# Loading and using the five row slices of w1 in the order 3, 4, 0, 1, 2 for the first chunk

## The chip, the cores and the metric

One core of one Trainium2 chip. The metric is the device time of a whole execution in microseconds (us). Profiles show the *span* from the first to the last instruction, which is about 1.8 us shorter than that time.

## The reference

```python
# x (1, 2048, 640), w1 (640, 1536), w2 (1536, 640), grad_out like x, all bf16
h   = x @ w1
out = silu(h) @ w2
# returned: out and the gradients of x, w1 and w2 for grad_out (by jax.vjp)
```

## The kernel before

The kernel takes x in four chunks of 512 rows. Per chunk it computes h (contraction over D = 640, that is, over five row slices of w1 with 128 rows each), silu and its derivative, out, and the gradients. Everything is bound by the matrix engine (TensorE); the only special place is the start, where w1 is still on its way from memory. For chunk 0 the code therefore works slice by slice: each slice of w1 that lands feeds 12 matmuls into six accumulators, for 256 of the 512 rows.

Loads, before anything else is awaited (`nc.sync` and `nc.scalar` are two queues that issue loads):

```python
early += [load_x(nc.sync, 0), load_x(nc.scalar, 1)]                     # 256 rows of x, natural layout
early += [load_w1(0, slice(0, F // 2)), load_w1(0, slice(F // 2, F), nc.scalar)]  # slice 0 in halves
early += [load_w1(k) for k in range(1, 3)]                              # slices 1, 2
for k in range(3, DT):                                                  # slices 3, 4
    load_w1(k)
nc.sync.dma_start_transpose(out=xT_next[:, :, HC:SC], in_=x2[HC:SC, :]) # the other 256 rows, transposed
# ... then w2, transposed grad_out, transposed w2 and w1, on the same queue
```

Transposing the first 256 rows on TensorE, and copying the five transposed column slices out in three pieces, on VectorE, ScalarE, VectorE:

```python
def pe_x(xT):
    slices = ((0, 1), (1, 3), (3, DT))
    tps = [ps_h.tile([P, hi - lo, 2, P], dt_in, ...) for lo, hi in slices]
    for q in range(2):
        for tp, (lo, hi) in zip(tps, slices):
            for dt_ in range(lo, hi):
                nc.tensor.transpose(tp[:, dt_ - lo, q, :], x_nat[:, q, dt_ * P:(dt_ + 1) * P], ident[:])
    for k, (tp, (lo, hi)) in enumerate(zip(tps, slices)):
        copy_tp = nc.scalar.copy if k % 2 else nc.vector.tensor_copy
        copy_tp(out=xT[:, lo:hi, 0:HC], in_=...)
```

The matmuls of chunk 0:

```python
def h_pair_mm(hp, pair, dt_, xT, cols, qs=(0, 1)):
    for q in qs:
        ft = 2 * pair + q
        nc.tensor.matmul(hp[:, q, :], lhsT=w1_nat[:, dt_, ft * P:(ft + 1) * P], rhs=xT[:, dt_, cols],
                         start=(dt_ == 0 and q == qs[0]), stop=(dt_ == DT - 1 and q == qs[-1]))

def h_first(xT, aT, ghT):
    pe_x(xT)
    ...
    for dt_ in range(DT):              # first 256 rows: slice by slice
        for pair in range(NPAIR):
            h_pair_mm(hs[0][pair], pair, dt_, xT, halves[0])
    ...                                # silu of the six accumulators
    for pair in range(NPAIR):          # other 256 rows: all slices have landed
        ...
        for q in range(2):
            for dt_ in range(DT):
                h_pair_mm(hp, pair, dt_, xT, halves[1], (q,))
```

Of the kernel before, what the change touches and what calls it, by code (L numbers as in the profile page):

```python
# [62 lines left out]
def kernel(  # L63
# [11 lines left out]
    nc = tc.nc  # L75
# [8 lines left out]
    F = w1.shape[1]  # L84
    ST, DT, FT = S // P, D // P, F // P
# [7 lines left out]
    NWARM = 18  # L93
    HC = 2 * P
    NPAIR = FT // 2
    NCOPY = 4
    dt_in = x.dtype

# [34 lines left out]
    with ExitStack() as mctx:  # L133
# [4 lines left out]
        tpool = mctx.enter_context(tc.tile_pool(name="tpool", bufs=3))  # L138
        hpool = mctx.enter_context(tc.tile_pool(name="hpool", bufs=NCOPY))
        opool = mctx.enter_context(tc.tile_pool(name="opool", bufs=2))  # L140

        warm = cpool.tile([P, P], dt_in, name="warm")
        early = [nc.vector.memset(warm[:], 1.0)]
# [25 lines left out]
        def load_x(eng, q):  # L169
            return eng.dma_start(out=x_nat[:, q, :], in_=x_v[:, q, :])  # L170

        def load_w1(k, cols=slice(0, F), eng=nc.sync):
            return eng.dma_start(out=w1_nat[:, k, cols], in_=w1_v[:, k, cols])  # L173

        early += [load_x(nc.sync, 0), load_x(nc.scalar, 1)]
        early += [load_w1(0, slice(0, F // 2)), load_w1(0, slice(F // 2, F), nc.scalar)]
        early += [load_w1(k) for k in range(1, 3)]
        for k in range(3, DT):
            load_w1(k)
        nc.sync.dma_start_transpose(out=xT_next[:, :, HC:SC], in_=x2[HC:SC, :])  # L180
        start_before_entry_wait(nc, {i.ins.name for i in early})
# [5 lines left out]
        nc.sync.dma_start_transpose(out=w1T[:], in_=w1[:, :])  # L187

        def pe_x(xT):
            slices = ((0, 1), (1, 3), (3, DT))  # L190
            tps = [ps_h.tile([P, hi - lo, 2, P], dt_in, name="tp", tag="hp") for lo, hi in slices]
            for q in range(2):
                for tp, (lo, hi) in zip(tps, slices):
                    for dt_ in range(lo, hi):
                        nc.tensor.transpose(
                            tp[:, dt_ - lo, q, :], x_nat[:, q, dt_ * P:(dt_ + 1) * P], ident[:]
                        )
            for k, (tp, (lo, hi)) in enumerate(zip(tps, slices)):
                copy_tp = nc.scalar.copy if k % 2 else nc.vector.tensor_copy
                copy_tp(out=xT[:, lo:hi, 0:HC], in_=tp[:].rearrange("p k q s -> p k (q s)"))  # L200
# [29 lines left out]
# [3 lines that stand above are left out]
                nc.tensor.matmul(  # L233
                    hp[:, q, :],
                    lhsT=w1_nat[:, dt_, ft * P:(ft + 1) * P],
                    rhs=xT[:, dt_, cols],
                    start=(dt_ == 0 and q == qs[0]),
                    stop=(dt_ == DT - 1 and q == qs[-1]),
                )

        def pair_silu(hp, pair, aT, cols):
            nc.scalar.activation(aT[:, 2 * pair:2 * pair + 2, cols], hp[:], ACT.Silu)

        def pair_grad(hp, pair, aT, ghT, cols):
            fts = slice(2 * pair, 2 * pair + 2)
            t = tpool.tile([P, 2, HC], FP32, name="t")
            nc.scalar.activation(t[:], hp[:], ACT.Tanh, scale=0.5)
            v = tpool.tile([P, 2, HC], dt_in, name="v")
            nc.vector.tensor_scalar(out=v[:], in0=t[:], scalar1=-0.5, scalar2=0.5, op0=ALU.mult, op1=ALU.add)
            nc.vector.scalar_tensor_tensor(  # L250
                out=ghT[:, fts, cols], in0=aT[:, fts, cols], scalar=1.0, in1=v[:],
                op0=ALU.subtract, op1=ALU.mult,
            )

        def h_first(xT, aT, ghT):
            pe_x(xT)
            halves = (slice(0, HC), slice(HC, SC))
            hs = [[ps_h.tile([P, 2, HC], FP32, name="hp") for _ in range(NPAIR)], []]
            for dt_ in range(DT):
                for pair in range(NPAIR):  # L260
                    h_pair_mm(hs[0][pair], pair, dt_, xT, halves[0])
            for pair in range(NPAIR):
                pair_silu(hs[0][pair], pair, aT, halves[0])
                if pair < NCOPY:
                    h_sb = hpool.tile([P, 2, HC], FP32, name="h_sb")
                    nc.vector.tensor_copy(out=h_sb[:], in_=hs[0][pair][:])
                    hs[0][pair] = h_sb
            grads = [(0, pair) for pair in list(range(NCOPY, NPAIR)) + list(range(NCOPY))]
            grads += [(1, pair) for pair in range(NPAIR)]
            for pair in range(NPAIR):  # L270
                hp = ps_h.tile([P, 2, HC], FP32, name="hp")
                hs[1].append(hp)
                for q in range(2):
                    for dt_ in range(DT):
                        h_pair_mm(hp, pair, dt_, xT, halves[1], (q,))
                pair_silu(hp, pair, aT, halves[1])
                if 1 <= pair <= 3:
                    half, done = grads.pop(0)
                    pair_grad(hs[half][done], done, aT, ghT, halves[half])
            for half, pair in grads:  # L280
                pair_grad(hs[half][pair], pair, aT, ghT, halves[half])
# [35 lines left out]
        for c in range(NCH):  # L317
# [15 lines left out]
            if c == 0:  # L333
                h_first(xT, aT, ghT)
                nc.sync.dma_start(
                    out=aT_scr[:, c * SC:(c + 1) * SC].rearrange("(ft p) s -> p ft s", p=P), in_=aT[:]
                )
                sd_phase(c, w2_nat, aT, oT_scr)
                for ft in range(FT):
                    g_group(ft, goT, ghT)  # L340
                nc.sync.dma_start(
                    out=ghT_scr[:, c * SC:(c + 1) * SC].rearrange("(ft p) s -> p ft s", p=P), in_=ghT[:]
                )
                sd_phase(c, w1T, ghT, gxT_scr)
                continue
# [20 lines left out]
    with ExitStack() as fctx:  # L366
# [17 lines left out]
        k = 0  # L384
        for fc in range(NFC):
            a_blk = a_blks[fc]
            g2T = fpool.tile([P, DT, FC], dt_in, name="g2T")
            for dt_ in range(DT):
                gp = ps_h.tile([P, FC], FP32, name="hp")
                for st in range(ST):  # L390
# [4 lines left out]
                        start=(st == 0),  # L395
                        stop=(st == ST - 1),
# [14 lines left out]
        k = 0  # L411
        for fc in range(NFC):
            gh_blk = gh_blks[fc]
            for dt_ in range(DT):
                if dt_ == DT // 2:
                    store_gw2(fc)
                if fc == NFC - 1 and dt_ == DT - 1:
                    for k, (lo, hi) in enumerate(((0, FC - P), (FC - P, FC))):
                        gp = ps_h.tile([P, FC], FP32, name="hp")
                        for st in range(ST):  # L420
# [4 lines left out]
                                start=(st == 0),  # L425
                                stop=(st == ST - 1),
# [12 lines left out]
                for st in range(ST):  # L439
# [4 lines left out]
                        start=(st == 0),  # L444
                        stop=(st == ST - 1),
# [38 lines left out]
```

## Time and profile before

| | value |
|---|---|
| time | 320.31 us, median of 3 runs (320.27 to 320.48) |
| span of the profiled run | 318.9 us |
| matmuls busy | 99% of the span |
| idle time of the matrix engine at w1 | 0.9 us in weight loads, all before 7.74 us |

The page's first part and its chain of waits, of the kernel before. In part 1 the columns are busy us, share of the span, number of instructions; PE is the matmuls of TensorE, PEld its weight loads, DVE VectorE, ACT ScalarE. The chain is what ended last, followed back to the start. (Names stand without numbers: `w_nat` is w1_nat or w2_nat, `hp` any accumulator.)

```profile
## 1 busy us (share of the span) xinstructions
PE 314.2 (99%) x1516; PEld 150.7 (47%) x1544; DVE 102.7 (32%) x182; ACT 76.8 (24%) x139; POOL 0.7 (0%) x6
...
## 4 chain that ended last, share of the span: by engine, by line
PE 96%; DMA 2%; issue 1%; SPq 0%; DVE 0%; DVEq 0%
PE hp L302 32%; PE hp L286 16%; PE hp L391 16%; PE hp L440 15%; PE hp L204 12%; PE hp L233 3%; DMA w_nat<-in_w_dram 2%; PE hp L421 1%; SPq L173 0%; SPq L170 0%; DVE g L432 0%; DVEq L432 0%; SPq L468 0%
```

So 96% of the span is TensorE one after another, and only 2% is a load, `w_nat<-in_w_dram`. Where that sits shows the chain of the first 20 us, in order of time (start us, duration us, what):

```profile
...
1.47 6.22 DMA w_nat<-in_w_dram
7.69 0.05 issue
7.74 10.65 PE hp L233 x96
...
```

The last thing that TensorE waited for was a load of w1 that landed at 7.69 us; from 7.74 us on the matmuls of h (L233) follow each other. The timeline of TensorE shows the pieces before that: first matmuls, then three groups of weight loads that each ended an idle time (in brackets: idle us, and what ended it).

```profile
...
2.59 1.25 PE L195 MATMUL tp<-ident,x_nat 128*128 128x128 bf16 x10
3.79 14.60 PE L233 MATMUL hp<-xT,w_nat 128*128 128x256 bf16 x120
...
```

```profile
...
3.53 1.22 PEld L233 LDWEIGHTS <-w_nat 128*128 128x128 bf16 x6
5.00 0.88 PEld L233 LDWEIGHTS <-w_nat 128*128 128x128 bf16 x6 [0.25 <-DMA w_nat<-in_w_dram]
6.18 1.21 PEld L233 LDWEIGHTS <-w_nat 128*128 128x128 bf16 x12 [0.30 <-DMA w_nat<-in_w_dram]
7.73 10.38 PEld L233 LDWEIGHTS <-w_nat 128*128 128x128 bf16 x96 [0.35 <-DMA w_nat<-in_w_dram]
...
```

The weight loads waited 0.25, 0.30 and 0.35 us for w1. The first of these was hidden: at that time matmuls started every 213 ns, where later they start every 109 ns, and the next one was not due yet. (The text below calls a step of 213 ns slow or half clock, and one of 109 ns full clock.) The other two are holes in the stream of matmuls.

### The profile page before, as it was taken

How to read it: one execution, taken by the hardware profiler on the slowest of the kernel's cores; microseconds unless marked ns; L12 is line 12 of the kernel's file. 1: busy time of each engine (PE TensorE's matmuls, PEld its weight loads, DVE VectorE, ACT ScalarE, POOL GpSimd, SP SyncE). 2: the span in 40 equal slices, each digit the busy share in tenths (PEclk: the TensorE clock that was granted, in tenths of full speed). 3: DMA queues.
4: the chain of work that ended last, by engine and by line, in shares of the span. 5: the costliest groups of instructions: out<-in, count | busy, mean ns of one | idle time of the engine just before them, and what ended most of it. 6: DMA issues, size and time to landing. Idle time of an engine off the chain costs nothing.

```text
span 318.9 us, 3632 instructions
## 1 busy us (share of the span) xinstructions
PE 314.2 (99%) x1516; PEld 150.7 (47%) x1544; DVE 102.7 (32%) x182; ACT 76.8 (24%) x139; POOL 0.7 (0%) x6
## 2 busy tenths in 40 slices
PE   9999999999999999999999999999999999999996
PEld 7854444444444444444444444444444444444443
DVE  1494641477410187710147741000000100001001
ACT  2691000644201354311064420111100001001100
POOL 0000000000000000000000000000000000000000
PEclk9999999999999999999999999999999999999999
DMA  8999999999999866492544089919999999996111
GB/s 268 311 177 222 216 266 255 313 270 304 260 232 342 201 191 174 144 299 82 164 120 128 0 268 265 210 38 290 222 258 255 228 214 339 229 311 216 38 39 45
DMA packets 147233, 67.02 MB, mean 210 GB/s; under 512 B 113937, under 2 KB 146705, under 8 KB 147217
## 3 DMA queue, kind: packets, MB, share of 16 engines
q1 hardware_dynamic: 146928, 66.43, 83.0%
q10 hardware_dynamic: 288, 0.36, 0.3%
q8 instruction: 12, 0.20, 0.3%
q14 instruction: 5, 0.03, 0.0%
HBM read 9.18 MB, written 28.97 MB: 120 GB/s over the span
## 4 chain that ended last, share of the span: by engine, by line
PE 96%; DMA 2%; issue 1%; SPq 0%; DVE 0%; DVEq 0%
PE hp L302 32%; PE hp L286 16%; PE hp L391 16%; PE hp L440 15%; PE hp L204 12%; PE hp L233 3%; DMA w_nat<-in_w_dram 2%; PE hp L421 1%; SPq L173 0%; SPq L170 0%; DVE g L432 0%; DVEq L432 0%; SPq L468 0%
## 5 line engine op out<-in xcount | busy, mean ns | idle before, releaser
L286 PE MATMUL hp<-goT,w2T 128*128 128x512 bf16 x239 | 56.8, 379 | 0.1
L302 PE MATMUL hp<-ghT,w1T 128*128 128x512 bf16 x235 | 52.2, 379 | 0.3
L302 PE MATMUL hp<-aT,w_nat 128*128 128x512 bf16 x234 | 52.1, 379 | 0.3
L391 PE MATMUL hp<-a_blk,go_nat 128*128 128x512 bf16 x235 | 51.7, 379 | 0.3
L440 PE MATMUL hp<-gh_blk,x_nat 128*128 128x512 bf16 x219 | 48.2, 379 | 0.3
L204 PE MATMUL hp<-xT,w_nat 128*128 128x512 bf16 x174 | 43.4, 379 | 0.3
L310 ACT ACTIVATE oT<-hp 128x512 bf16<-128x512 f32 x24 | 14.5, 604 | 106.8 <-PE hp L302 106.8
L302 PEld LDWEIGHTS <-w1T 128*128 128x128 bf16 x240 | 23.5, 98 | 28.3
L391 PEld LDWEIGHTS <-go_nat 128*128 128x128 bf16 x240 | 23.5, 98 | 28.3
L286 PEld LDWEIGHTS <-w2T 128*128 128x128 bf16 x240 | 23.5, 98 | 28.3
L302 PEld LDWEIGHTS <-w_nat 128*128 128x128 bf16 x240 | 23.5, 98 | 28.1
L293 DVE SCALAR_TENSOR_TENSOR ghT<-ghT,hp 128x512 bf16<-128x512 bf16 x48 | 32.5, 681 | 7.3 <-PE hp L286 7.3
L440 PEld LDWEIGHTS <-x_nat 128*128 128x128 bf16 x224 | 21.9, 98 | 26.4
L312 DVE CAST oT<-hp 128x512 bf16<-128x512 f32 x16 | 11.1, 691 | 72.2 <-PE hp L302 67.7
L213 ACT ACTIVATE aT<-hp 128x512 bf16<-128x512 f32 x36 | 21.5, 597 | 30.4 <-PE hp L204 30.4
L204 PEld LDWEIGHTS <-w_nat 128*128 128x128 bf16 x180 | 17.6, 98 | 21.3
L220 DVE SCALAR_TENSOR_TENSOR ghT<-aT,v 128x512 bf16<-128x512 bf16 x36 | 24.6, 684 | 0.2
L219 DVE TENSOR_SCALAR v<-t 128x512 bf16<-128x512 f32 x36 | 15.4, 426 | 26.7 <-ACT t L217 26.7
L217 ACT ACTIVATE t<-hp 128x512 f32<-128x512 f32 x36 | 21.3, 592 | 0.0
L451 DVE CAST g<-hp 128x512 bf16<-128x512 f32 x7 | 4.8, 691 | 47.0 <-PE hp L440 34.5
L401 DVE CAST g2T<-hp 128x512 bf16<-128x512 f32 x7 | 4.8, 692 | 46.1 <-PE hp L391 46.1
L399 ACT ACTIVATE g2T<-hp 128x512 bf16<-128x512 f32 x8 | 4.8, 597 | 47.0 <-PE hp L391 47.0
(28 smaller groups left out, 77.3 us busy)
## 6 DMA issues: line engine op xcount, KB each, us to landing
aT_scr<-aT SPq DMA_DIRECT2D x4, 1536.0 KB, 6.3
ghT_scr<-ghT SPq DMA_DIRECT2D x4, 1536.0 KB, 8.2
out_dram<-o_sb SPq DMA_DIRECT2D x8, 640.0 KB, 3.3
oT_scr<-oT SPq DMA_DIRECT2D x4, 640.0 KB, 3.6
go_nat<-in_grad_out_dram SPq DMA_DIRECT2D x4, 640.0 KB, 8.3
gxT_scr<-oT SPq DMA_DIRECT2D x4, 640.0 KB, 4.7
w_nat<-in_w_dram SPq DMA_DIRECT2D x1, 1920.0 KB, 11.1
x_nat<-in_x_dram SPq DMA_DIRECT2D x3, 640.0 KB, 7.2
```

The source lines that it names most:

```text
L204: nc.tensor.matmul(hp[:], lhsT=w1_nat[:, dt_, ft * P:(ft + 1) * P], rhs=xT[:, dt_, :], start=(dt_ == 0), stop=(dt_ == DT - 1),)
L213: nc.scalar.activation(aT[:, ft, :], hp[:], ACT.Silu)
L217: nc.scalar.activation(t[:], hp[:], ACT.Tanh, scale=0.5)
L219: nc.vector.tensor_scalar(out=v[:], in0=t[:], scalar1=-0.5, scalar2=0.5, op0=ALU.mult, op1=ALU.add)
L220: nc.vector.scalar_tensor_tensor(out=ghT[:, ft, :], in0=aT[:, ft, :], scalar=1.0, in1=v[:], op0=ALU.subtract, op1=ALU.mult)
L286: nc.tensor.matmul(gp[:], lhsT=w2T[:, dt_, ft * P:(ft + 1) * P], rhs=goT[:, dt_, :], start=(dt_ == 0), stop=(dt_ == DT - 1),)
L293: nc.vector.scalar_tensor_tensor(out=ghT[:, ft, :], in0=ghT[:, ft, :], scalar=1.0, in1=gp[:], op0=ALU.add, op1=ALU.mult)
L302: nc.tensor.matmul(op_[:], lhsT=w_all[:, ft, dt_ * P:(dt_ + 1) * P], rhs=rhs_all[:, ft, :], start=(ft == 0), stop=(ft == FT - 1),)
L310: nc.scalar.activation(oT[:, dt_, :], op_[:], ACT.Copy)
L312: nc.vector.tensor_copy(out=oT[:, dt_, :], in_=op_[:])
L391: nc.tensor.matmul(gp[:], lhsT=go_nat[:, st, dt_ * P:(dt_ + 1) * P], rhs=a_blk[:, st, :], start=(st == 0), stop=(st == ST - 1),)
L440: nc.tensor.matmul(gp[:], lhsT=x_nat[:, st, dt_ * P:(dt_ + 1) * P], rhs=gh_blk[:, st, :], start=(st == 0), stop=(st == ST - 1),)
```

## The change

The intent: use the slices of w1 in another order, and load them in that same order. Loads, transposes and matmuls of chunk 0 follow `KORD`; later chunks do not change. With it, the sizes of the copies of transposed x change from 1, 2, 2 slices to 1, 1, 3.

```diff
+    KORD = (3, 4, 0, 1, 2)
@@ loads
-        early += [load_w1(0, slice(0, F // 2)), load_w1(0, slice(F // 2, F), nc.scalar)]
-        early += [load_w1(k) for k in range(1, 3)]
-        for k in range(3, DT):
+        early += [load_w1(KORD[0], slice(0, F // 2)), load_w1(KORD[0], slice(F // 2, F), nc.scalar)]
+        early += [load_w1(k) for k in KORD[1:3]]
+        for k in KORD[3:]:
             load_w1(k)
@@ pe_x
-            slices = ((0, 1), (1, 3), (3, DT))
+            slices = ((3, 4), (4, DT), (0, 3))
@@ h_pair_mm
-                    start=(dt_ == 0 and q == qs[0]),
-                    stop=(dt_ == DT - 1 and q == qs[-1]),
+                    start=(dt_ == KORD[0] and q == qs[0]),
+                    stop=(dt_ == KORD[-1] and q == qs[-1]),
@@ h_first, both loops
-            for dt_ in range(DT):
+            for dt_ in KORD:
```

More of the change, by code (lines that the diff above doesn't have):

```diff
@@ L273, in h_first @@
                 for q in range(2):
-                    for dt_ in range(DT):
+                    for dt_ in KORD:
                         h_pair_mm(hp, pair, dt_, xT, halves[1], (q,))
```

## The prediction

> **What bounds it now.** TensorE. The page's first part has matmuls busy 314.2 of 318.9 us (99%); the chain of waits that ended last is 96% TensorE, 2% loads of w1, 1% issue. In the steady parts 128x512 matmuls start every 216 ns. Only the first 8 us, where w1 arrives, can be touched by this change.
>
> **The start, read from the timeline.** The first matmul of h starts at 3.79 us, released by a 128x256 VectorE copy (3.45 to 3.74). Matmuls with 256 columns then start every 213 ns until about 5.5 us and every 109 ns afterwards. The Trainium skill ("TensorE: Matmul & The Clock Gate", Back-to-back issue gap) gives N/1.2 ns cold and N/2.4+2.5 ns warm, 213 and 109 ns at N = 256: the trace agrees. From the 16 completions of each load (same skill, "DMA: Bandwidth & Descriptors", Why a DMA increments its semaphore by 16: it is complete only when the last engine has reported), the pieces of w1 in order of issue landed at 3.46, 4.96, 6.14, 7.69, 8.63 and 9.65 us. The weight loads waited 0.25, 0.30 and 0.35 us; in matmul starts the two real holes are 5.89 to 6.18 and 7.40 to 7.74, that is 0.19 and 0.23 us beyond the usual 109 ns: 0.42 us in all. Slices four and five are wanted at about 9.05 and 10.36 us and landed 0.4 and 0.7 us before. From 7.74 us TensorE runs without a hole.
>
> **What the change does.** It renames. Loads keep sizes, order, queues and semaphores; the first slice consumed is still the first loaded. The instruction streams differ in four places only:
> - ScalarE's copy of transposed x shrinks from two slices (0.58 us) to one (estimate, scaled: 0.3 to 0.4 us). It is needed at 6.18 us and ended at 4.24: off the path.
> - VectorE's second copy grows from two slices (0.42 us) to three. From 0.29 us for 256 and 0.42 for 512 columns I estimate 0.55 us for 768, so it ends near 4.43 instead of 4.30 us.
> - The matmuls' wait for that copy moves from slice position four to three (two places), wanted at 7.74 us: slack of 3.3 us.
>
> The ten transposes, the first VectorE copy and hence the start at 3.79 us stay. VectorE and ScalarE are idle between 4.3 and 10.8 us.
>
> **On the critical path:** 0 us by construction. What can vary is which HBM rows are read when, and how the slowest of 16 engines falls; this can only move the 0.42 us of holes, or open one at slices four and five. A later full clock would partly be swallowed by the same holes.
>
> **Prediction.** 320.3 us, 319.9 to 320.7 with 8 chances in 10. Faster by over 2%: 0.005; within 2%: 0.99; slower by over 2%: 0.005. Two per cent is 6.4 us, many times what this stage holds in holes.
>
> **Right** if: first h matmul near 3.8 us; two holes of 0.2 to 0.3 us before positions two and three, none before four and five; landings within 0.5 us of those above; VectorE's copy of 128x768 ends before 4.6 us and nobody waits for it; from 8 us on both traces coincide after a shift. **Wrong** if weight loads wait over 0.5 us more or less for w1, or a matmul waits for VectorE's copy.
>
> **What would make it wrong.** If the position of a slice in HBM decides how fast it arrives, the holes could vanish (-0.4 us) or grow by as much; or the transposed load behind w1 could land after 11.7 us (it landed at 10.92) and stall the second half.

## More of the kernel before

The record gives each run a state, fast or slow. Timings compare fast runs with fast runs, and the one kernel whose state is unknown is marked.

## The result, and the profile after

| | before | after |
|---|---|---|
| median us | 320.53 (320.27 to 321.48, 6 runs) | 320.88 (320.27 to 321.18, 6 runs) |
| ratio | | 1.0005, 95% interval 0.9989 to 1.0021: the same |
| span of the profiled run | 318.9 us | 318.5 us |

Ratios here are the mean time of one kernel's fast runs over that of the other's in the same rounds, so not quite the ratio of the medians that are quoted. 320.88 lies 0.18 us above the upper end of the predicted range, but the unchanged kernel had risen as well: its six runs are the three that the prediction started from (320.27, 320.31, 320.48) and three more (320.58, 320.83, 321.48). The ratio applied to the 320.31 that the prediction started from is 320.5.

The page after, the same two parts (line numbers are one higher than before):

```profile
## 1 busy us (share of the span) xinstructions
PE 315.3 (99%) x1544; PEld 150.9 (47%) x1544; DVE 102.9 (32%) x182; ACT 76.6 (24%) x139; POOL 0.7 (0%) x6
...
## 4 chain that ended last, share of the span: by engine, by line
PE 98%; DMA 1%; DVE 0%; issue 0%; DVEq 0%; SPq 0%
PE hp L303 33%; PE hp L287 16%; PE hp L392 16%; PE hp L441 15%; PE hp L205 12%; PE hp L234 4%; PE hp L422 1%; DMA x_nat<-in_x_dram 1%; PE tp L196 0%; DVE g L433 0%; DVEq L433 0%; SPq L469 0%
```

The first 20 us of its chain:

```profile
...
2.70 1.25 PE tp L196 x10
3.95 14.02 PE hp L234 x120
...
```

The timeline of its matmuls, then of its weight loads:

```profile
...
2.70 1.25 PE L196 MATMUL tp<-ident,x_nat 128*128 128x128 bf16 x10
3.91 14.06 PE L234 MATMUL hp<-xT,w_nat 128*128 128x256 bf16 x120
...
```

```profile
...
3.77 13.91 PEld L234 LDWEIGHTS <-w_nat 128*128 128x128 bf16 x120
...
```

In this profile no load of w1 is in the chain and no weight load waited: all 120 run from 3.77 us as one group. The first matmul came 0.11 us later than in the profile before, the last of the 120 started 0.43 us earlier (17.69 against 18.12 us), and the span is 0.43 us shorter. Read alone, that looks like a small success: the holes are gone. But the timed runs of the same kernel show no gain. The profiled run after (320.27 us) was the fastest of its six, and the profiled run before (320.73 us) was slower than all three that were timed with it, so the pair of profiles flatters the change. There were two readings to tell apart.

The copies did as the change says. Groups of VectorE by shape, from 3 to 4.8 us after the change (busy us, mean ns, idle us before it):

```profile
L201 DVE COPY xT<-tp 128x768 bf16<-128x768 bf16 x1 | 0.6, 557 | 0.1
L201 DVE COPY xT<-tp 128x256 bf16<-128x256 bf16 x1 | 0.3, 292 | 3.1 <-PE tp L196 3.1
```

The copy of three slices took 557 ns where that of two had taken 424 ns; it ended at 4.55 us, its consumer was due at 7.32 us, and nobody waited for it.

### The profile page after: what moved, and what is told of

It reads as the page before. It is cut to its first block, busy times and chain, and to the rows that moved or that the text cites. A ratio compares the mean times of both kernels' runs of the same rounds, so it can differ in the third digit from the quotient of the medians.

```text
span 318.5 us, 3660 instructions
## 1 busy us (share of the span) xinstructions
PE 315.3 (99%) x1544; PEld 150.9 (47%) x1544; DVE 102.9 (32%) x182; ACT 76.6 (24%) x139; POOL 0.7 (0%) x6
## 4 chain that ended last, share of the span: by engine, by line
PE 98%; DMA 1%; DVE 0%; issue 0%; DVEq 0%; SPq 0%
PE hp L303 33%; PE hp L287 16%; PE hp L392 16%; PE hp L441 15%; PE hp L205 12%; PE hp L234 4%; PE hp L422 1%; DMA x_nat<-in_x_dram 1%; PE tp L196 0%; DVE g L433 0%; DVEq L433 0%; SPq L469 0%
```

## The experiments

**Theory 1:** the order is a renaming. The holes come from loads that land late by chance, whatever rows they carry, and differ from run to run. **Theory 2:** rows 3, 4, 0 arrive sooner because of where they lie in memory; the 0.43 us is real and drowned in the scatter of the timings. **Theory 3:** the larger copy costs something.

All results were correct except those of the kernel that is wrong.

### 1. The unchanged kernel again, as a control

No edit.

> The kernel before, unchanged, as a control. Theory 1 (the order is only a renaming; the holes before slices two and three come and go with chance from run to run): time ratio 1.000 within 0.2%; landings of the pieces of w1 differ from those of the first profile of before by some tenths of a us, and the holes before positions two and three (0.19 and 0.23 us) come out at another size. The span after the first matmul that uses w2 (300.69 us in both profiles so far) stays within 0.05 us, so that all scatter between runs comes from the first 18 us. Theory 2 (rows 3, 4, 0 of w1 arrive sooner because of where they lie in HBM): the two holes are there again, 0.3 to 0.5 us together, and landings of positions two and three stay near 6.1 and 7.7 us.

Measured: ratio 1.0008 (0.9997 to 1.0020), 321.37 us against 321.10 for the very same code. Its profile (who waited for whom in the first 19 us: total us, times, longest):

```profile
...
PEld L233 <- DMA w_nat<-in_w_dram: 1.7, 3, 0.9
PE hp L233 <- DMA w_nat<-in_w_dram: 0.8, 2, 0.7
...
```

Weight loads waited 1.7 us instead of 0.9, and the hole before the second slice alone was 0.8 us beyond the usual step (0.19 in the first profile); the one before the third slice was gone. The slice in the second place landed at 6.88 us, not near 6.1. The two holes of the first profile are thus not a property of the kernel, against theory 2. The 1.7 us are as far from the first profile as the changed kernel's 0 is, the other way.

### 2. The changed kernel again, twice

No edit.

> The changed kernel again. Theory 1: ratio 1.000 within 0.2%; the profile need not be free of holes this time. Theory 2: again no hole, slices two and three land near 5.5 and 7.0 us, and the first matmul with w2 starts 0.4 us earlier than in the kernel before; ratio about 0.9987.

Measured: ratio 1.0007 (0.9991 to 1.0023). The profile that theory 2 wanted free of holes has some again. Its waits in the first 19 us:

```profile
...
PEld L234 <- DMA w_nat<-in_w_dram: 1.7, 2, 1.0
PE hp L234 <- DMA w_nat<-in_w_dram: 1.0, 2, 0.5
...
```

Its chain:

```profile
...
0.99 6.14 DMA w_nat<-in_w_dram
7.18 11.96 PE hp L234 x108
...
```

Its timeline of matmuls:

```profile
...
3.63 1.44 PE L234 MATMUL hp<-xT,w_nat 128*128 128x256 bf16 x6
5.60 1.15 PE L234 MATMUL hp<-xT,w_nat 128*128 128x256 bf16 x6 [0.53 <-DMA w_nat<-in_w_dram]
7.18 11.96 PE L234 MATMUL hp<-xT,w_nat 128*128 128x256 bf16 x108 [0.43 <-DMA w_nat<-in_w_dram]
...
```

The load of w1 is back in the chain; the slice in second place landed at 7.13 us, 1.6 us later than in the other profile of the same kernel (5.52), and the span is 319.7 us instead of 318.5.

> The changed kernel once more, to narrow the interval. Renaming theory: ratio 1.000 within 0.15%. If the changed order has a real cost of 0.05 to 0.07% (the two ratios so far were 1.0005 and 1.0007, not clear of 1), it shows again. The profile has again holes of some size between 0 and 2 us, the span after the first matmul with w2 is 300.69 us.

Measured: ratio 1.0005 (0.9976 to 1.0034); no hole this time, slices two and three landed at 5.68 and 7.25 us. Three profiles of one kernel: no hole, 1.7 us of waiting weight loads, no hole. All three ratios lie slightly above 1, but so does that of the control, 1.0008, which is the same code; no cost of the change can be read from them. The gain that theory 2 expected, a ratio of 0.9987, lies outside two of the three intervals (0.9989 to 1.0021 and 0.9991 to 1.0023) and inside the widest.

### 3. Only the sizes of the copies

```diff
-            slices = ((0, 1), (1, 3), (3, DT))
+            slices = ((0, 1), (1, 2), (2, DT))
```

> Slices of w1 in the old order, but transposed x copied out as one, one and three slices, as the change does. Theory 1: ratio 1.000 within 0.2%, nobody waits for the 128x768 copy. Theory 2: as the kernel before, holes of 0.3 to 0.5 us. A third theory (the larger copy on VectorE costs something): slower by its growth of 0.13 us at most, with a wait for it at slice three.

Measured: ratio 1.0002 (0.9990 to 1.0014). The 128x768 copy took 558 ns, ended at 4.45 us and nobody waited for it: theory 3 falls. Waits for w1 were 1.3 us in two places, at the first slice and its second half, where theory 1 allows them and theory 2 does not foresee them.

### 4. Another order, 4, 3, 2, 1, 0

```diff
-    KORD = (3, 4, 0, 1, 2)
+    KORD = (4, 3, 2, 1, 0)
-            slices = ((3, 4), (4, DT), (0, 3))
+            slices = ((4, DT), (3, 4), (0, 3))
```

> Order 4, 3, 2, 1, 0 for loads and use. Theory 1: ratio 1.000 within 0.2%, landings by position spread as in the other kernels. Theory 2: a different pattern of landings, which follows the slices and not the positions: slices 1 and 2 late (they were the late ones in the kernel before), now at positions four and three.

Measured: ratio 1.0013 (1.0000 to 1.0027), waits of 0.9 us, at the second half of the first slice and at the second slice. Landings followed the positions (6.44, 7.34, 8.30, 9.28 us for the second to the fifth): slices 2 and 1, said to be late, were not late in their new places. The interval touches 1.0000, as the control's nearly does; with identical code at 1.0008 I take it as the same.

### 5. Half of the change at a time

Loads in the new order, use in the old one; and the reverse of that. Both compute the right result, since every matmul waits for the slice that it reads.

```diff
@@ load_only: KORD in the loads alone
+        early += [load_w1(KORD[0], slice(0, F // 2)), load_w1(KORD[0], slice(F // 2, F), nc.scalar)]
+        early += [load_w1(k) for k in KORD[1:3]]
@@ use_only: KORD in pe_x, h_pair_mm and h_first alone
+            slices = ((3, 4), (4, DT), (0, 3))
+            for dt_ in KORD:
```

> Half of the change: w1 is loaded in the order 3, 4, 0, 1, 2 but used in the order 0 to 4, with transposes as before. Result is correct. All theories: the first matmul of h waits for the slice in the third place of the load order, so it starts when that lands, at 6.9 to 7.9 us instead of 3.6 to 4.3; the holes after it vanish, since the rest has landed by then. The later stages only shift, so the span is the start of the first matmul with w2 plus 300.69 us. If the array keeps its full clock through the idle time that start is 7.4 plus 120 matmuls at 109 ns, about 20.5 us (2 to 2.5 us longer than the kernel before); if the idle time brings back half the clock for 20 to 30 matmuls, 2 to 3 us more. Time 323 to 327 us.

> The other half: loads in the order 0 to 4, use and transposes in the order 3, 4, 0, 1, 2. Result is correct. The first matmul of h waits for the fourth place of the load order, 8.0 to 8.8 us, the second slice for the fifth, about 9.7 us. About 3 to 3.5 us longer than before at full clock, 2 to 3 us more if the clock falls back: 324 to 328 us.

Measured: ratio 1.0124 (1.0106 to 1.0141), 324.94 against 320.81 us, for the loads alone; 1.0160 (1.0143 to 1.0177), 326.11 us, for the use alone. The timelines of TensorE, first the loads alone, then the use alone:

```profile
...
7.39 15.62 PE L234 MATMUL hp<-xT,w_nat 128*128 128x256 bf16 x120 [3.61 <-DMA w_nat<-in_w_dram]
...
```

```profile
...
8.39 15.62 PE L234 MATMUL hp<-xT,w_nat 128*128 128x256 bf16 x120 [4.59 <-DMA w_nat<-in_w_dram]
...
```

The first matmul waited for the third and the fourth place of the load order, which landed at 7.34 and 8.34 us, at once as expected. So the stage can cost microseconds, and what the change must keep is that loads and use agree; it keeps that, hence nothing happens. After the wait, 22 matmuls started at 213 ns before the step became 109 ns: 22 times 104 ns is 2.3 us. The profile before has 8 such steps as well, so some 1.4 us of the 4 and 5 us are slow steps that came on top of the later start (3.6 and 4.6 us); the holes at w1, now gone, offset 0.3 to 0.4 us.

### 6. What the waits cost: none left

All 60 matmuls of the first 256 rows read the first half slice of w1 only. The result is wrong.

```diff
-                    lhsT=w1_nat[:, dt_, ft * P:(ft + 1) * P],
+                    lhsT=w1_nat[:, 0, ft % 6 * P:(ft % 6 + 1) * P] if one else w1_nat[:, dt_, ft * P:(ft + 1) * P],
@@ h_first, first loop
-                h_pair_mm(hs[0][pair], pair, dt_, xT, halves[0])
+                h_pair_mm(hs[0][pair], pair, dt_, xT, halves[0], one=True)
```

> The loads are unchanged, but all 60 matmuls of the first half multiply by columns of the first half slice of w1 alone (wrong result on purpose), so that no wait for w1 is left after the first one; it shows what the waits between matmuls cost in an ordinary run. Theory 1 (waits for late pieces are there in nearly every run, their size by chance): 0.5 to 1.0 us faster than the kernel before, ratio 0.997 to 0.9985, and less scatter between runs than its 1.1 us. Theory 2 (the waits are a matter of which slices come when): the same 0.4 us that the changed kernel gained in its first profile.

Measured: ratio 0.9988 (0.9974 to 1.0002): 0.4 us, less than theory 1 expected, with an interval that just includes 1, and scatter of 0.9 us that did not shrink much. The waits suggest why:

```profile
...
PEld L302 <- DMA w_nat<-in_w_dram: 0.4, 1, 0.4
PEld L233 <- DMA xT<-in_x_dram: 0.3, 1, 0.3
...
```

TensorE arrived earlier at the next loads of the same queue and waited there instead: 0.3 us for the transposed second half of x, 0.4 us for w2 (0.21 and 0.24 us beyond the usual step, in matmul starts). But in this profile TensorE was early for a second reason too: only 2 steps were slow, against 8 in the profile before, which is 0.6 us. With 8 slow steps (an estimate from its own steps) it would have wanted both loads after they had landed, at 10.84 and 17.64 us. So this one profile does not show that the waits move on in an ordinary run. What the other profiles show is a limit: in the seven of sections 1 to 4 and of the first pair, w2 had landed only 0.4 to 0.9 us before the first matmul that used it, so holes that cost more than that could not have been won back in full without making the stream earlier.

In timed runs the holes at w1 are worth about 0.1%, with an interval from 0.26% down to nothing. More than that an order of the slices could hardly have brought.

### 7. Do the loads behind w1 disturb it?

In the nine profiles so far that load whole slices, packets of w1 (3 KB each, 512 of them, 0.121 us in the median) included 6 to 16 that took 0.45 to 1.9 us (the text below says 4 to 16, since it counts the halved loads too), nearly all between 3 and 6 us. At that time the queue prepares the transposed load of x (issue at 2.9 us). Here every load behind w1 is held back until the first activation of h, by one-element copies into its target:

```diff
+                if pair == 0:
+                    firsts = [xT[0:1, 0, HC:HC + 1], w2_nat[0:1, 0, 0:1], goT_first[0:1, 0, 0:1], ...]
+                    for first in firsts:
+                        nc.scalar.copy(out=first, in_=aT[0:1, 0, 0:1])
+                    late_loads(xT)     # the same loads, moved here
```

> Loads of x and w1 as before; all loads behind them on the queue (transposed x, w2, transposed gradient and weights) are held back until the first activation of aT by one-element copies into their targets, which those loads then overwrite. Result is correct; the kernel is some 8 to 12 us slower, which is not the question. In the ten profiles so far, of the 512 packets of 3 KB of w1 that take 0.121 us as a rule, 4 to 16 took over 0.45 us (up to 1.9 us), nearly all between 3 and 6 us, just when the queue of SyncE makes up the transposed load of x. If that makes the late packets, then here there are none or one, and the slice in the second place lands at 5.0 to 5.3 us, as the middle one of its 16 completions did in all profiles. If they come anyhow (chance in the memory, or the start of the stream itself), there are again 4 to 16 and a landing anywhere from 5.4 to 7.1 us.

Measured: one run of 326.5 us (state unknown; only its first 7 us matter here). 12 packets took over 0.45 us, and the second slice landed at 6.37 us though the middle one of its 16 completions came at 4.87. So this theory of mine falls, as far as one profile can show it: the late packets come with no transposed load issued before 11.9 us. It was 5 us slower, not 8 to 12. What makes these packets late stays open.

### 8. Slices two and three in halves

If single late packets decide, a smaller piece with a completion of its own should be in time more often.

```diff
-        early += [load_w1(k) for k in range(1, 3)]
+        early += [load_w1(k, h) for k in range(1, 3) for h in (slice(0, F // 2), slice(F // 2, F))]
```

> Order as before, but the slices in the second and third place are loaded as two column halves each, with a completion of their own, so that six matmuls need only the half. If lateness of single pieces by chance is the cost, then 0.2 to 0.5 us faster (ratio 0.9985 to 0.9995), with smaller holes before the second place. If it is the rows of w1 or the whole bandwidth of the stream, no change beyond 0.1 us; two more issues at 0.43 us each could even make slices four and five late.

> The kernel with slices two and three loaded as halves again. Its first timing gave 0.9992 with one run at 322.8 us that made the interval wide. If the halves help: ratio 0.998 to 0.999, most runs below the median of the kernel before. If not: 1.000 and again scatter of a us or more.

> Slices in the second and third place loaded as halves, in the changed order 3, 4, 0, 1, 2. The halves alone gave ratios of 0.9992 (0.9966 to 1.0017) and 0.9967 (0.9944 to 0.9990). If the order of the slices does not matter and the halves are worth something, this lies between them, 0.997 to 0.999, in a third sample. If the changed order had a cost or a gain of its own, it would show as a shift against those two; a ratio at 1.000 or above would mean that the second of the two was a lucky sample (its profile ran at full clock from the first matmul of h on[...]). The span after the first matmul with w2 stays 300.68 us.

Measured: 0.9992 (0.9966 to 1.0017), 0.9967 (0.9944 to 0.9990), and in the changed order 0.9967 (0.9923 to 1.0010). Medians 320.46, 320.01 and 319.93 us against 320.81, 321.16 and 321.19. In none of the three profiles did a matmul wait at slices two or three. All three ratios are below 1 but only one interval is clear of it, and two of the three sets hold an outlier (322.80 and 322.93 us). The second ratio lies below what was expected (0.998 to 0.999), the third at the lower edge of it (0.997 to 0.999). The halves are probably some 0.2% faster (mean of the three ratios 0.9975); that is the only correct version that seems to beat both kernels, and it does so in either order of the slices. That is more than the kernel without waits gained. The landings say how it could be: the whole stream was earlier, not only the halves. The fourth slice landed at 7.70, 7.99 and 7.55 us (7.99 to 9.00 in the 11 profiles with whole slices), the transposed half of x at 10.09, 10.37 and 9.92 us (10.26 to 11.27 in the ten of those where that load was not moved). Fewer packets were late as well (4, 2 and 5 of w1's packets over 0.45 us, against 6 to 16, though most of them are now half as large). Why, no run shows.

Nor do the profiles show that the earlier stream made the gain. Against the first profile of the kernel before, the first matmul with w2 came 0.00, 0.90 and 1.05 us earlier, and 0.1, 0.84 and 0.73 us of that are slow steps saved (7, 0 and 1 of them against 8). TensorE ran at full clock from 3.92 and 4.41 us on in the last two; in the five profiles of the kernel before and the changed one that began between 5.57 and 6.37 us. Whether this is luck in two profiles, or comes with the halves in most runs, is open: the other timed runs have no trace.

### All landings together

A load reports 16 completions in the trace. The table shows when the 8th and the 16th (last) completion of the slice in second place came, by load order.

| order of loads | kernels | 8th of 16, us | last, us |
|---|---|---|---|
| 0, 1, 2, 3, 4 | before, control, copies, use alone, no wait, loads late | 5.02, 5.13, 4.83, 4.80, 4.89, 4.87 | 6.14, 6.88, 6.03, 5.42, 5.83, 6.37 |
| 3, 4, 0, 1, 2 | after, again, third, loads alone | 4.86, 5.03, 4.94, 4.82 | 5.52, 7.13, 5.68, 6.21 |
| 4, 3, 2, 1, 0 | reverse | 5.13 | 6.44 |

The middle of a load is nearly always at the same time, 4.8 to 5.1 us. The last completion wanders over 1.7 us. Its mean is 6.11 us for the old order (six profiles) and 6.13 us for the new one (four): no sign that the rows matter, though with so few profiles and such a spread these means alone could hide a few tenths of a us; the ratios above are the stronger evidence. And in all 14 profiles the span minus the start of the first matmul that uses w2 is 300.67 to 300.70 us, from spans of 317.9 to 324.7. From that matmul on nothing varies; the whole scatter between profiles is made at the start.

The holes are not all of that scatter. In the 11 profiles without a gap of several us, the start of that first matmul (17.18 to 18.98 us) is the sum of the start of the first matmul of h (3.63 to 4.31 us), 120 steps of 109 ns, 104 ns more for each slow step (0 to 9 of them, up to 0.94 us), and the remaining idle time (0.1 to 1.6 us). The end of the slow steps is a term of its own, as large as the holes of the first profile, and the theories above leave it out.

## Why the prediction was right or wrong

- *"TensorE bounds, only the first 8 us can be touched"*: right. The constant 300.68 us behind the start shows it.
- *"0 us on the critical path by construction"*: right. Three ratios of 1.0005, 1.0007 and 1.0005 stand beside 1.0008 for unchanged code, and each half of the change alone costs 4 to 5 us, so that the agreement of both orders is what matters. That the mechanism was right, and not only the number, rests on these runs.
- *Costs of the copies*: right. VectorE estimated 0.55 us, measured 0.557; ScalarE estimated 0.3 to 0.4, measured 0.37; neither was awaited.
- *"Two holes of 0.2 to 0.3 us before positions two and three ... landings within 0.5 us"*: wrong as a sign. In the first profile both holes were gone and landings came up to 0.7 us earlier; in the second the weight loads waited 1.7 us. By the letter, "weight loads wait over 0.5 us more or less for w1" said that the prediction had failed, while the time had not moved. The step that failed is taking the holes of one profile as a property of the kernel; the control moved by as much without any edit.
- *"If the position of a slice in HBM decides how fast it arrives"*: was named as the risk; the landings (6.11 against 6.13 us) and the reverse order speak against it.
- *The range, 319.9 to 320.7*: too narrow. It was 0.8 us wide and rested on three runs within 0.21 us of each other. The 50 runs of the kernel before, these three included, go from 320.08 to 323.52 us (on several chips), and eight in ten of them lie between 320.42 and 321.57. So the three were low ones. That nothing would change held; the term for scatter was the mis-sized one.
- The 0.43 us that the profile after showed was real for that run and chance for the kernel. Taking all the holes away, in the kernel without waits, brought 0.4 us (by the interval, 0.8 us to nothing). In its one profile TensorE waited at x and w2 instead, but an early full clock had helped it to get there.

## What to carry to other kernels

Renaming which piece comes first did nothing here, since loading and using agreed; one order without the other cost the whole lateness of the piece and more slow steps, 4 to 5 us. A wait that ends with a load is a sample: before a hole of some tenths of a us is explained or celebrated, profile the unchanged kernel a second time, compare the profiled run's own time with the median, and count the slow steps at the start of each profile. If a stream of loads is late as a whole, removing one wait on it can move the wait to the next load. Smaller pieces with their own completion at the front of the stream are the only lever that seemed to work here, by about 0.2%, and what made that gain is not shown.

## What the Trainium skill lacked or had wrong

- "DMA: Bandwidth & Descriptors", "Why a DMA increments its semaphore by 16", is right that only the last of the 16 tells that data are there, but gives no size for the spread. Here the 8th completion of a 384 KB load came at 4.8 to 5.1 us in 11 profiles and the 16th at 5.4 to 7.1 us.
- "HBM Reference", section Latency, gives 0.2 us on average and 2 us at high load. With only this core's loads in view, 6 to 16 of 512 packets of 3 KB took 0.45 to 1.9 us, at a median of 0.12 us (11 profiles). A packet's time is not the same thing as the latency of one access, so this neither confirms nor refutes the figures. The page does not say when in a stream slow accesses fall; of these packets nearly all that were late began between 3 and 6 us, and no run here shows the cause.
- "DMA: Bandwidth & Descriptors", section Bandwidth, advises to batch loads to 1 MiB or more; its table is for loads issued from GpSimd, and the section has no figure for loads of this size queued one behind the other on SyncE. Here such slices of 384 KB landed at 7.69, 8.63 and 9.65 us in the kernel before, 0.98 us apart on average, which is about 400 GB/s (an estimate from these times), and halves of 192 KB did no harm (ratios 0.9967 to 0.9992).
- "TensorE: Matmul & The Clock Gate", section Part 1, says that the array falls back to half clock after an idle window of about 3.4 us and that the moment of full clock varies. The runs agree: after 3.94 us of idle time in the kernel with late loads, 15 steps between matmuls of 256 columns were 213 or 214 ns again, where they had been 109 (the first few after the gap were still 109). The number of slow steps at the start was 0 to 9 in the 11 profiles without such a gap. A case that the page does not have: after that gap the granted clock in the profile fell too (0.57 from 16 to 20 us), but at the start it did not. It was 1.00 from 0 to 4 and from 4 to 8 us of the kernel before, where 8 steps were slow; the trace's record of the clock begins only at 5.66 us, when the steps become fast. So at the start half clock is to be read from the steps between matmuls.
